# Query tiles of a linear-attention and expert kernel: TensorE's transposes ahead of the projection, ScalarE's exponentials ahead of the projection's copy

## The chip, the cores and the metric

The kernel runs on one core of one Trainium2 chip. The metric is the time of one execution in microseconds. Before the change three runs gave 260.74 us in the median (260.23 to 260.80).

## What is computed

Attention with random features, then a layer of experts. The reference, cut to the part that the change is in:

```python
def phi(x):                                   # x: q or k, scaled; omega is 128 x 64
    proj = np.einsum('bhsd,md->bhsm', x, omega)
    h = proj - np.sum(x * x, axis=-1, keepdims=True) / 2.0
    h = h - np.max(h, axis=-1, keepdims=True)
    return np.exp(h) / np.sqrt(m)
kv  = np.einsum('bhsm,bhsd->bhmd', k_p, v)    # and z, the sum of k_p
num = np.einsum('bhsm,bhmd->bhsd', q_p, kv)
den = np.einsum('bhsm,bhm->bhs', q_p, z)[..., None] + 1e-06
x   = num / den                               # 2304 rows of 8 heads * 64
# then: gate x @ w_gate, one expert of 8 per row, relu(x @ w1[e]) @ w2[e] * gate
```

Sizes: 4 batches, 8 heads, 576 rows each, 128 features; 8 experts, 512 to 1024 to 512.

## The kernel before, in words

One loop (L773) runs 18 key steps (`n < NK`), then 18 query tiles of 128 rows (`t` = 0 to 17), and three more steps in which the last tiles drain. The schedule is manual: on each engine instructions stand in the order in which the Python code issues them, and an engine that waits holds up all that stands behind it. After the loop come the experts: three passes of products each for `relu(x @ w1)` and for `@ w2`, with the operands split into a high and a low part, one expert block after another.

A query tile `t` goes through four steps of the loop:

- Step t. TensorE projects q with omega (`project`, called at L795, matmuls at L177; "P" below): 16 matmuls into two banks of PSUM, heads 4 to 7 in `pj[1]`, heads 0 to 3 in `pj[0]`. VectorE takes maxima of `pj[1]` (L194, called at L863). ScalarE copies `pj[0]` into the SBUF tile `d` (L862), VectorE takes the maxima of that copy (L194, called at L865), GpSimd subtracts them in `d` (L866), and ScalarE writes heads 4 to 7 less their maxima into `d` (L882, four instructions).
- Step t + 2. TensorE transposes `d` (L809, 16 matmuls with the identity; "T" below) into two banks, 3 and 4, under the name `qtr`. ScalarE takes the exponential of each bank (L873, two instructions) into `qpT`.
- Step t + 3. TensorE multiplies `qpT` with the keys' sums `kv_sb` (`numer`, L689, 32 matmuls; "N" below) into `qacc`. This is one pair of banks (tag `a2`, one buffer), so N of the next tile may not begin before VectorE has read this one. `normalise` does that: `den` (L715), a sum of gate products of the tile before (L724), the reciprocal (L718), the product into `xr` (L721). A DMA on SyncE's queue stores `xr` (L727).

So in step t TensorE runs P of tile t, T of tile t - 2, N of tile t - 3, in this order. ScalarE runs copy (t), exponentials (t - 2), L882 (t). VectorE runs maxima of `pj[1]` (t), maxima of `d` (t), `normalise` (t - 3), and in steps 10 to 17 also one transpose of expert rows (`turn_x`, L439). GpSimd subtracts and splits the first expert's weights (L137, L142).

In steps 0 to 5 the last keys' sums are still being finished: `project` first runs a small pair of transposes that waits in the list `beside` (L301, `ktr`), which ScalarE copies out (L305, `kvT`), and after some N a few matmuls give `kv_sb`'s gate columns (L314, copied by VectorE at L322). Such background work hangs on generators that `run(...)` moves on; where a generator yields no name, any `run` call moves it.

The banks that the projection, the transposes and the numerator use (L783, L792, L800, L829):

```python
def pair(name):
    return ps.tile([128, 1024], F32, tag="a2", name=name, bufs=1)
pj = [bank((2 * t + i) % 3, f"pjq{n}{i}") for i in range(2)]
trs = [bank((3 + i, (2, SM)[i])[t > NT], f"qtr{n}{i}") for i in range(2)]
whole = pair(f"qacc{t}")
```

Of the kernel before, what the change touches and what calls it, by code (L numbers as in the profile page):

```python
# [9 lines left out]
F32 = mybir.dt.float32  # L10
# [3 lines left out]
AF = mybir.ActivationFunctionType  # L14
# [5 lines left out]
B, H, S, D, M = 4, 8, 576, 64, 128  # L20
N, DM, E, FF = B * S, H * D, 8, 1024
NP = H // 2
NT = N // 128
# [42 lines left out]
def attention_moe(ctx, tc, kT, qT, va, om, wg, w1, w2, cap, ident, tri, desc, lst, tab0, out):  # L66
    nc = tc.nc
# [12 lines left out]
    def bank(i, name):  # L80
        return ps.tile([128, 512], F32, tag=f"b{i}", name=name, bufs=1)
# [4 lines left out]
    SM = 5  # L86
# [4 lines left out]
    id_sb = const.tile([128, 128], F32, name="id_sb")  # L91
# [61 lines left out]
    def run_one(task):  # L153
        try:
            task[1] = next(task[0])
        except StopIteration:
            tasks.remove(task)

    def run(at=None, times=1, most=99):
        for _ in range(times):  # L160
            for task in list(tasks):
                if task[1] is None or (task[1] == at and most > 0):
                    most -= task[1] is not None
                    run_one(task)
# [9 lines left out]
    def project(parts, banks):  # L174
        def one(k, i):
            rows = slice(64 * i, 64 * i + 64)
            nc.tensor.matmul(banks[i][:, k * M : (k + 1) * M], parts[k][rows, :], om_s[rows, :], start=True, stop=True)  # L177

        a = 0
        if beside:  # L180
            a, small_t = beside.pop(0)
            small_t()
        n = len(parts)
        one(0, 1 - a)
        for k in range(1, n):
            one(k - 1, a)
            one(k, 1 - a)
        one(n - 1, a)
# [16 lines left out]
    qp = qstack.enter_context(tc.tile_pool(name="qpool", bufs=2, side="right"))  # L205
# [564 lines left out]
    ex_l, d_l, qT_l, acc_l = {}, {}, {}, {}  # L770
    step = [0]

    for n in range(NK + NT + 3):  # L773
        t = step[0] = n - NK
        mx = small.tile([128, H], F32, tag="mx", name=f"mx{n}", bufs=4) if n < NK + NT else None

        if n < NK:
            keys = [chunks[b, g][0][:, u * 128 : (u + 1) * 128] for b, g, u in KU[KG * n : KG * n + KG]]
            if n == 0:

                pj = [bank(i, f"pjk{n}{i}") for i in range(4)]
                project(keys[0:2], pj[0:2])
                project(keys[2:4], pj[2:4])  # L783
            else:

                if n == 1:
                    pj = [bank(SM, "pjk10"), pair("pjk11")[:, 0:512]]
                else:
                    pj = [bank(2 * (n % 2) + i, f"pjk{n}{i}") for i in range(2)]
                project(keys, pj)  # L790
        elif t < NT:
            pj = [bank((2 * t + i) % 3, f"pjq{n}{i}") for i in range(2)]  # L792
            c = max(i for i in range(len(QB) - 1) if QB[i] <= t)
            o = (t - QB[c]) * 128
            project([qc[c][:, p, o : o + 128] for p in range(NP)], pj)  # L795
        run("T")

        if 0 <= t - 2 < NT:
            d = d_l.pop(t - 2)
            trs = [bank((3 + i, (2, SM)[i])[t > NT], f"qtr{n}{i}") for i in range(2)]  # L800

            parts = [
                [(trs[i][:, u * 64 : (u + 1) * 64], d[64 * i : 64 * i + 64, u, :], i) for u in range(H)] for i in range(2)
            ]

            for x in chain(*zip_longest(*parts)):
                if x is not None:
                    rows = slice(64 * x[2], 64 * x[2] + 64)
                    nc.tensor.transpose(x[0], x[1], id_sb[rows, rows])  # L809
        if t == NT:  # L810
            h0 = h_tiles()
        run()

        if 0 <= n - 2 < NK:
            ex = ex_l.pop(n - 2)
            for k, (b, g, u) in enumerate(KU[KG * (n - 2) : KG * (n - 1)]):
                if u == 0:
                    if acc_l.get("kp") is None:
                        acc_l["kp"] = pair("kp")
                    acc_l[0] = bank(4, f"kacc{b}{g}") if g == 0 else acc_l["kp"]  # L820
                kv_acc(b, g, u, ex, k, acc_l[0])
                if u == 8:
                    start(kv_gate(b, g, acc_l[0]))
        elif 0 <= t - 3 < NT:
            acc_l["kp"] = whole = None
            if t in (NT, NT + 2):
                acc_l[0] = [bank(3 * (t > NT) + i, f"qacc{t}{i}") for i in range(2)]
            else:
                whole = pair(f"qacc{t}")  # L829
                acc_l[0] = [whole[:, 0:512], whole[:, 512:1024]]  # L830
            numer(t - 3, qT_l.pop(t - 3), acc_l[0])
        run("N")
        if t == NT + 2:
            turn[0] = 2
            take = mm1(*AHEAD[0], *h0, "i0")

        if n < NK:
            ex = kp.tile([128, H, M], F32, tag="ex", name=f"ex{n}", bufs=3)

            for o, q in ((0, pj[0:2]), (2, pj[2:4])) if n == 0 else ((0, pj),):  # L840
                w = KG // (len(pj) // 2)
                maxima_of(mx, o, units(q[0])[:, 0:w, :])
                run()
                feeds(n, 0, mx[:, o : o + 1])
                for k in range(w):
                    nc.scalar.activation(  # L846
                        ex[:, o + k, :], q[0][:, k * M : (k + 1) * M], AF.Exp, bias=mx[:, o + k : o + k + 1], scale=1.0
                    )
                maxima_of(mx, 4 + o, units(q[1])[:, 0:w, :])
                run()  # L850
                feeds(n, 1, mx[:, 4 + o : 5 + o])
                h = slice(4 + o, 4 + o + w)
                nc.vector.tensor_tensor(
                    ex[:, h, :], units(q[1])[:, 0:w, :], mx[:, h].unsqueeze(2).to_broadcast([128, w, M]), op=ALU.add
                )
                nc.scalar.activation(ex[:, h, :], ex[:, h, :], AF.Exp)
            ex_l[n] = ex
            run()
        else:
            if t < NT:  # L860
                d = qp.tile([128, H, M], F32, tag="d", name=f"d{t}", bufs=3)
                nc.scalar.copy(d[:, 0:4, :], units(pj[0]))  # L862
                maxima(mx, 1, units(pj[1]))  # L863
                run()
                maxima(mx, 0, d[:, 0:4, :])  # L865
                nc.gpsimd.tensor_tensor(d[:, 0:4, :], d[:, 0:4, :], spread(mx, 0), op=ALU.add)  # L866
                feeds(n, 0, mx[:, 0:1])
                d_l[t] = d
            run("P", times=2, most=0 if t == 17 else 1 if t in EARLY_SPLIT or t == 16 else 2)
            if 0 <= t - 2 < NT:  # L870
                qpT = qp.tile([128, 2, H * 64], F32, tag="qpT", name=f"qpT{t}", bufs=2)
                for i in range(2):
                    nc.scalar.activation(qpT[:, i, :], trs[i], AF.Exp)  # L873
                qT_l[t - 2] = qpT
                run()
            if t == NT + 2:
                take()
            if t > NT:
                split_x()
            if t < NT:  # L880
                for k in range(4):
                    nc.scalar.activation(  # L882
                        d[:, 4 + k, :], pj[1][:, k * M : (k + 1) * M], AF.Identity, bias=mx[:, 4 + k : 5 + k], scale=1.0
                    )
                run()
            for task in [x for x in tasks if x[1] == "G"]:
                run_one(task)
            if 0 <= t - 3 < NT:
                normalise(t - 3, acc_l[0], whole)
                if t == 3:  # L890
                    start(first_item())
            if t in EARLY_AT:
                b0 = EARLY_AT.index(t)
                turn_x(b0, b0 + 1, b0)
            if t in EARLY_SPLIT:
                split_early(EARLY_SPLIT.index(t))
            if t in (NT, NT + 1):

                b0 = NBA + 5 * (t - NT)
                split_x = turn_x(b0, b0 + 5, b0 - NBA, nc.gpsimd)  # L900
            run(times=3)
        run("E")

        if n == NK + 1:
            kstack.close()
            open_experts()
        if n == 3:
            start(setup())
        if t in (5, 6):
            load_x(slice(0, 32 * NBA), 0, NBA, range(2 * t - 10, 2 * t - 8))  # L910
        if t in FIRST_LOAD:
            i = 2 * FIRST_LOAD.index(t)
            load_x(slice(32 * NBA, SLOTS), NBA, NB, range(i, i + 2))
# [318 lines left out]
```

## Time and profile before

| | before |
|---|---|
| median of 3 runs | 260.74 us (260.23 to 260.80) |
| the profiled execution | 259.68 us, its span 257.9 us |
| TensorE busy | 252.2 us (98%) |
| its weight loads | 231.4 us (90%) |
| VectorE, ScalarE, GpSimd busy | 165.9, 147.7, 49.4 us |
| granted TensorE clock, mean | 0.997 of 2.4 GHz |

The query tiles take the stretch from about 46 to 100 us of the span; the experts follow. An engine's busy time counts an instruction from its start to its last write; the next one on the engine can start before that, so the distance between two starts is what an instruction takes of its engine, and it is often shorter than its duration. In the timeline a row is one instruction or a few alike in a row, with start, duration and, in brackets, how long the engine stood idle before it and what ended that.

### The profile page before, as it was taken

How to read it: one execution, taken by the hardware profiler on the slowest of the kernel's cores; microseconds unless marked ns; L12 is line 12 of the kernel's file. 1: busy time of each engine (PE TensorE's matmuls, PEld its weight loads, DVE VectorE, ACT ScalarE, POOL GpSimd, SP SyncE). 2: the span in 40 equal slices, each digit the busy share in tenths (PEclk: the TensorE clock that was granted, in tenths of full speed). 3: DMA queues.
4: the chain of work that ended last, by engine and by line, in shares of the span. 5: the costliest groups of instructions: out<-in, count | busy, mean ns of one | idle time of the engine just before them, and what ended most of it. 6: DMA issues, size and time to landing. Idle time of an engine off the chain costs nothing. (4 is left out here: it accounts for less than half of the span.)

```text
span 257.9 us, 7657 instructions
## 1 busy us (share of the span) xinstructions
PE 252.2 (98%) x3042; PEld 231.4 (90%) x3042; DVE 165.9 (64%) x355; ACT 147.7 (57%) x370; POOL 49.4 (19%) x95
## 2 busy tenths in 40 slices
PE   7999999999999999999999999999999999999993
PEld 6999999999999999999988889999888999988882
DVE  2999888779899999554853656566750064667500
ACT  3888878899999995327301645552361155524511
POOL 1015111243989986200000000000000000000000
PEclk9999999999999999999999999999999999999998
DMA  7998997544788657790079527992013998850221
GB/s 216 397 325 252 333 341 207 180 123 140 242 247 270 202 202 243 252 346 1 0 150 293 178 84 252 228 274 92 3 42 101 291 215 270 271 159 0 61 85 44
DMA packets 37507, 49.06 MB, mean 190 GB/s; under 512 B 2578, under 2 KB 24722, under 8 KB 37458
## 3 DMA queue, kind: packets, MB, share of 16 engines
q1 hardware_dynamic: 36338, 46.91, 59.8%
q10 hardware_dynamic: 1120, 1.52, 1.8%
q8 instruction: 28, 0.46, 0.7%
q14 instruction: 21, 0.17, 0.2%
HBM read 36.49 MB, written 11.93 MB: 188 GB/s over the span
## 5 line engine op out<-in xcount | busy, mean ns | idle before, releaser
L742 PE MATMUL hi<-xhi,w1hi 128*128 128x256 f32 (+1 forms) x192 | 56.7, 295 | 0.0
L743 PE MATMUL hi<-xhi,w1lo 128*128 128x256 f32 (+1 forms) x192 | 56.4, 294 | 0.0
L744 PE MATMUL hi<-xlo,w1hi 128*128 128x256 f32 (+1 forms) x192 | 56.3, 293 | 0.0
L755 DVE SCALAR_TENSOR_TENSOR hlo<-hi,hhi 128x256 fp32r<-128x256 f32 x48 | 20.2, 420 | 43.1 <-ACT hr L753 21.7
L753 ACT ACTIVATE hhi<-hi 128x256 fp32r<-128x256 f32 x48 | 18.4, 385 | 36.7 <-PE hi L744 36.7
L927 PE MATMUL yi<-w2hi,hhi 128*128 128x512 f32 x96 | 37.4, 390 | 0.0
L928 PE MATMUL yi<-w2hi,hlo 128*128 128x512 f32 x96 | 37.4, 389 | 0.0
L742 PEld LDWEIGHTS hi<-xhi,w1hi 128*128 128x128 f32 x192 | 36.0, 188 | 0.3
L743 PEld LDWEIGHTS hi<-xhi,w1lo 128*128 128x128 f32 x192 | 36.0, 188 | 0.1
L744 PEld LDWEIGHTS hi<-xlo,w1hi 128*128 128x128 f32 x192 | 36.0, 187 | 0.0
L194 DVE TENSOR_REDUCE mx<-pjk 128x4 f32<-128x512 f32 (+1 forms) x38 | 23.4, 656 | 4.2 <-PE pjk L177 4.2
L846 ACT ACTIVATE ex<-pjk,mx 128x128 f32<-128x128 f32 x72 | 20.7, 368 | 5.9 <-DVE mx L194 5.6
L177 PE MATMUL pjk<-om_s,kraw 64*128 64x128 f32 x288 | 23.6, 297 | 0.4 <-DMA kraw<-kT 0.3
L439 DVE STREAM_TRANSPOSE xt<-xg 128x128 f32<-128x128 f32 (+3 forms) x16 | 19.3, 1205 | 7.0 <-DMA xg<-x_d 7.0
L933 PE MATMUL yi<-w2lo,hhi 128*128 128x512 f32 x96 | 23.7, 389 | 0.0
L689 PE MATMUL qacc<-kv_sb,qpT 128*64 128x73 f32 x576 | 22.5, 230 | 0.0
L177 PEld LDWEIGHTS pjk<-om_s,kraw 64*128 64x128 f32 x288 | 20.0, 200 | 1.7 <-DMA kraw<-kT 0.6
L927 PEld LDWEIGHTS yi<-w2hi,hhi 128*128 128x128 f32 x96 | 18.0, 188 | 3.8 <-issue 0.2
L933 PEld LDWEIGHTS yi<-w2lo,hhi 128*128 128x128 f32 x96 | 18.0, 188 | 3.7
L866 POOL TENSOR_TENSOR d<-d,mx 128x512 f32<-128x512 f32 x18 | 18.7, 1041 | 13.4 <-DVE mx L194 9.8
L928 PEld LDWEIGHTS yi<-w2hi,hlo 128*128 128x128 f32 x96 | 18.0, 188 | 3.6
L882 ACT ACTIVATE d<-pjq,mx 128x128 f32<-128x128 f32 x72 | 21.0, 404 | 0.3 <-DVE mx L194 0.3
(154 smaller groups left out, 420.7 us busy)
## 6 DMA issues: line engine op xcount, KB each, us to landing
w1raw<-w SPq DMA_DIRECT2D x16, 512.0 KB, 7.8
w2raw<-w SPq DMA_DIRECT2D x16, 512.0 KB, 4.7
x_d<-xr SPq DMA_DIRECT2D x18, 256.0 KB, 3.2
xg<-x_d SPq DMA_DIRECT2D x12, 288.0 KB, 8.1
v<-va SPq DMA_DIRECT2D x8, 325.0 KB, 4.5
kraw<-kT SPq DMA_DIRECT2D x8, 288.0 KB, 5.5
out<-ysi SPq DMA_DIRECT2D x9, 256.0 KB, 2.1
v<-va SPq DMA_DIRECT2D x3, 650.0 KB, 7.0
```

Source lines behind the costliest of these rows:

```text
L177: nc.tensor.matmul(banks[i][:, k * M : (k + 1) * M], parts[k][rows, :], om_s[rows, :], start=True, stop=True)
L194: nc.vector.tensor_reduce(mx[:, a : a + src.shape[1]], src, op=ALU.max, axis=AX.X, negate=True)
L689: nc.tensor.matmul(acc[i][r : r + 64, p * ROW : (p + 1) * ROW], qpT[:, r // 64, (4 * i + p) * 64 : (4 * i + p) * 64 + 64], kv_sb[(t * 128 ...
L742: nc.tensor.matmul(pt, whi_[:, k, fs], xhi[:, k, sl], start=(k == 0), stop=False)
L743: nc.tensor.matmul(pt, wlo_[:, k, fs], xhi[:, k, sl], start=False, stop=False)
L744: nc.tensor.matmul(pt, whi_[:, k, fs], xlo[:, k, sl], start=False, stop=(k == 3))
L755: nc.vector.scalar_tensor_tensor(lo, src, 0.0, hi.bitcast(F32), op0=ALU.max, op1=ALU.subtract)
L846: nc.scalar.activation(ex[:, o + k, :], q[0][:, k * M : (k + 1) * M], AF.Exp, bias=mx[:, o + k : o + k + 1], scale=1.0)
L882: nc.scalar.activation(d[:, 4 + k, :], pj[1][:, k * M : (k + 1) * M], AF.Identity, bias=mx[:, 4 + k : 5 + k], scale=1.0)
L927: nc.tensor.matmul(pt, hhi[:, f, sl], w2_at(w_hi, f), start=(f == 0), stop=False)
L928: nc.tensor.matmul(pt, hlo[:, f, sl], w2_at(w_hi, f), start=False, stop=False)
L933: nc.tensor.matmul(pt, hhi[:, f, sl], w2_at(w_lo, f), start=False, stop=(f == 7))
```

## The change

In each step of a query tile the 16 transposes are issued ahead of the projection, and the two exponentials ahead of ScalarE's copy of the projection. The call of `run()` behind the exponentials goes.

```diff
         mx = small.tile([128, H], F32, tag="mx", name=f"mx{n}", bufs=4) if n < NK + NT else None
 
+        if 0 <= t - 2 < NT:
+            d = d_l.pop(t - 2)
+            trs = [bank((3 + i, (2, SM)[i])[t > NT], f"qtr{n}{i}") for i in range(2)]
...
+                    nc.tensor.transpose(x[0], x[1], id_sb[rows, rows])
         if n < NK:
...
             project([qc[c][:, p, o : o + 128] for p in range(NP)], pj)
         run("T")
 
-        if 0 <= t - 2 < NT:
-            d = d_l.pop(t - 2)
...
-                    nc.tensor.transpose(x[0], x[1], id_sb[rows, rows])
         if t == NT:
...
         else:
+            if 0 <= t - 2 < NT:
+                qpT = qp.tile([128, 2, H * 64], F32, tag="qpT", name=f"qpT{t}", bufs=2)
+                for i in range(2):
+                    nc.scalar.activation(qpT[:, i, :], trs[i], AF.Exp)
+                qT_l[t - 2] = qpT
             if t < NT:
                 d = qp.tile([128, H, M], F32, tag="d", name=f"d{t}", bufs=3)
                 nc.scalar.copy(d[:, 0:4, :], units(pj[0]))
...
             run("P", times=2, most=0 if t == 17 else 1 if t in EARLY_SPLIT or t == 16 else 2)
-            if 0 <= t - 2 < NT:
-                qpT = qp.tile([128, 2, H * 64], F32, tag="qpT", name=f"qpT{t}", bufs=2)
-                for i in range(2):
-                    nc.scalar.activation(qpT[:, i, :], trs[i], AF.Exp)
-                qT_l[t - 2] = qpT
-                run()
             if t == NT + 2:
```

TensorE at the seam between steps 5 and 6, before: the last transposes of step 5, its numerator, the first matmuls of step 6's projection (`pjq`: projection, `qtr`: transposes, `qacc`: numerator).

```order
L809 MATMUL qtr_1285<-id_sb,d_1159 128x64
L809 MATMUL qtr_1286<-id_sb,d_1159 128x64
L689 MATMUL qacc_1303<-kv_sb_72,qpT_1245 64x73 x16
L177 MATMUL pjq_1344<-om_s,qhlo 128x128
L177 MATMUL pjq_1343<-om_s,qhlo 128x128
```

The same place in the changed kernel:

```order
L177 MATMUL pjq_1289<-om_s,qhhi 128x128
L177 MATMUL pjq_1290<-om_s,qhhi 128x128
L689 MATMUL qacc_1303<-kv_sb_72,qpT_1237 64x73 x16
L788 MATMUL qtr_1343<-id_sb,d_1240 128x64
L788 MATMUL qtr_1344<-id_sb,d_1240 128x64
```

The numerator now stands straight behind the projection, and a step opens with the transposes.

ScalarE in steps 2 and 3, the first two with transposes, before (`d<-pjq ... 128x512`: the copy, `qpT`: the exponentials, `d<-pjq,mx`: L882):

```order
L305 COPY kvT_1030<-ktr_1062 128x2x64
L862 COPY d_1096<-pjq_1060 128x512
L873 ACTIVATE qpT_1101<-qtr_1074 128x512
L873 ACTIVATE qpT_1101<-qtr_1075 128x512
L882 ACTIVATE d_1096<-pjq_1061,mx_1059 128x128 x4
L305 COPY kvT_1030<-ktr_1112 128x2x64
L862 COPY d_1159<-pjq_1110 128x512
L873 ACTIVATE qpT_1164<-qtr_1124 128x512
L873 ACTIVATE qpT_1164<-qtr_1125 128x512
L882 ACTIVATE d_1159<-pjq_1111,mx_1109 128x128 x4
```

The same place in the changed kernel:

```order
L305 COPY kvT_1030<-ktr_1080 128x2x64
L863 ACTIVATE qpT_1096<-qtr_1060 128x512
L863 ACTIVATE qpT_1096<-qtr_1061 128x512
L867 COPY d_1099<-pjq_1078 128x512
L881 ACTIVATE d_1099<-pjq_1079,mx_1059 128x128 x4
L305 COPY kvT_1030<-ktr_1130 128x2x64
L863 ACTIVATE qpT_1159<-qtr_1110 128x512
L863 ACTIVATE qpT_1159<-qtr_1111 128x512
L867 COPY d_1162<-pjq_1128 128x512
L881 ACTIVATE d_1162<-pjq_1129,mx_1109 128x128 x4
```

The copy has moved behind both exponentials; the copies of `kvT` still stand first. The instructions of VectorE, GpSimd and SyncE stand in the same order in both kernels, row for row.

## Rows read from the trace of the kernel before

**Rows 1.** The page's busy times; the list of TensorE's waits (total, times, longest)

```profile
PE 252.2 (98%) x3042; PEld 231.4 (90%) x3042; DVE 165.9 (64%) x355; ACT 147.7 (57%) x370; POOL 49.4 (19%) x95
...
PE pjk L177 <- DMA kraw<-kT: 0.3, 1, 0.3
```

**Rows 2.** Windows: busy us (instructions) by engine, clock, DMA share, GB/s, steps 6 to 10

```profile
61.80:75.85 14.05, 14.05 (x332) 13.32 (x328) 12.33 (x31) 12.90 (x36) 10.77 (x13) 1.00 0.82 248
```

**Rows 3.** Timeline of TensorE, step 9: start, us, engine, line, operation

```profile
70.32 1.16 PE L177 MATMUL pjq<-om_s,qhlo 64*128 64x128 f32 x16
71.32 0.66 PE L809 MATMUL qtr<-id_sb,d 64*128 64x64 f32 x16
71.91 1.25 PE L689 MATMUL qacc<-kv_sb,qpT 128*64 128x73 f32 x32
```

**Rows 4.** Timeline of ScalarE, step 9

```profile
71.64 0.59 ACT L862 COPY d<-pjq 128x512 f32<-128x512 f32 x1 [0.16 <-PE pjq L177]
72.12 1.09 ACT L873 ACTIVATE qpT<-qtr 128x512 f32<-128x512 f32 x2
73.08 1.16 ACT L882 ACTIVATE d<-pjq,mx 128x128 f32<-128x128 f32 x4
```

**Rows 5.** Timeline of VectorE, from step 8's normalise to step 9's

```profile
70.44 0.17 DVE L715 TENSOR_SCALAR den<-qacc 128x8 f32<-128x8 f32 x1 [0.26 <-PE qacc L689]
...
70.88 0.77 DVE L721 TENSOR_TENSOR xr<-qacc,rec 128x584 f32<-128x584 f32 x1
71.59 0.69 DVE L194 TENSOR_REDUCE mx<-pjq 128x4 f32<-128x512 f32 x1
72.25 0.69 DVE L194 TENSOR_REDUCE mx<-d 128x4 f32<-128x512 f32 x1
73.20 0.17 DVE L715 TENSOR_SCALAR den<-qacc 128x8 f32<-128x8 f32 x1 [0.26 <-PE qacc L689]
```

**Rows 6.** Timeline of VectorE and TensorE, step 5: a numerator that follows `xr`

```profile
59.76 0.77 DVE L721 TENSOR_TENSOR xr<-qacc,rec 128x584 f32<-128x584 f32 x1
...
59.94 0.72 PE L809 MATMUL qtr<-id_sb,d 64*128 64x64 f32 x15
60.67 1.25 PE L689 MATMUL qacc<-kv_sb,qpT 128*64 128x73 f32 x32
```

**Rows 7.** Timeline of ScalarE, steps 2 and 3

```profile
52.02 0.29 ACT L305 COPY kvT<-ktr 128x128 f32<-128x128 f32 x1
52.20 0.60 ACT L862 COPY d<-pjq 128x512 f32<-128x512 f32 x1
...
53.66 1.16 ACT L882 ACTIVATE d<-pjq,mx 128x128 f32<-128x128 f32 x4
54.66 0.31 ACT L305 COPY kvT<-ktr 128x128 f32<-128x128 f32 x1
54.81 0.65 ACT L862 COPY d<-pjq 128x512 f32<-128x512 f32 x1
```

**Rows 8.** Timeline of VectorE, step 3, and TensorE's numerator in step 4

```profile
55.49 0.69 DVE L194 TENSOR_REDUCE mx<-d 128x4 f32<-128x512 f32 x1 [0.50 <-ACT d L862]
56.10 0.15 DVE L715 TENSOR_SCALAR den<-qacc 128x8 f32<-128x8 f32 x1
...
56.52 0.77 DVE L721 TENSOR_TENSOR xr<-qacc,rec 128x584 f32<-128x584 f32 x1
...
57.51 1.25 PE L689 MATMUL qacc<-kv_sb,qpT 128*64 128x73 f32 x32
```

**Rows 9.** Timeline, step 12: VectorE's extra transpose; step 9's subtraction on GpSimd

```profile
82.61 0.41 DVE L439 STREAM_TRANSPOSE xt<-xg 128x128 f32<-128x128 f32 x1
...
74.06 1.04 POOL L866 TENSOR_TENSOR d<-d,mx 128x512 f32<-128x512 f32 x1
```

**Rows 10.** Timeline of ScalarE and TensorE, steps 17 and 18

```profile
94.21 1.09 ACT L873 ACTIVATE qpT<-qtr 128x512 f32<-128x512 f32 x2
...
95.18 0.89 PE L809 MATMUL qtr<-id_sb,d 64*128 64x64 f32 x16
```

More of the change, by code (lines that the diff above doesn't have):

```diff
@@ L775, in attention_moe @@
         mx = small.tile([128, H], F32, tag="mx", name=f"mx{n}", bufs=4) if n < NK + NT else None
+        if 0 <= t - 2 < NT:
+            d = d_l.pop(t - 2)
+            trs = [bank((3 + i, (2, SM)[i])[t > NT], f"qtr{n}{i}") for i in range(2)]
+            parts = [
+                [(trs[i][:, u * 64 : (u + 1) * 64], d[64 * i : 64 * i + 64, u, :], i) for u in range(H)] for i in range(2)
+            ]
+            for x in chain(*zip_longest(*parts)):
+                if x is not None:
+                    rows = slice(64 * x[2], 64 * x[2] + 64)
+                    nc.tensor.transpose(x[0], x[1], id_sb[rows, rows])
         if n < NK:
@@ L796, in attention_moe @@
         run("T")
-        if 0 <= t - 2 < NT:
-            d = d_l.pop(t - 2)
[L800 to L808, printed above, removed]
-                    nc.tensor.transpose(x[0], x[1], id_sb[rows, rows])
         if t == NT:
```

## Prediction

> **What bounds the kernel now.** I read the page first, then TensorE's waits, then the timelines of one step. TensorE is busy 252.2 of 257.9 us, and the longest wait its list names after the start is 0.3 us, for a load [rows 1]. So the end moves by what TensorE loses or gains, and I follow the four engines through one query step to see which of the others could hold it up.
>
> Step 9 is typical. TensorE starts the projection P at 70.32, the transposes T at 71.32, the numerator N at 71.91 [rows 3]. P therefore takes 1.00 us of the engine and T 0.59. One step lasts 2.76 us, from one `den` to the next (73.20 - 70.44) [rows 5], which leaves N 1.17. ScalarE's copy comes 1.32 us after P's start, having waited for P [rows 4]; the two exponentials take 0.96 (73.08 - 72.12). VectorE starts the maxima of `pj[1]` at 71.59, 1.27 after P, those of the copy 0.61 after the copy's start, then idles 0.26 until N, which had begun 1.29 before, lets `den` go; `xr` starts 0.44 after `den` (70.88 - 70.44) [rows 4, 5].
>
> The tight place is `qacc`, a single pair of banks: N may not begin before `xr` of the tile before has been read out. Step 5 shows the price of that hand-over: fifteen of the sixteen transposes begin at 59.94 and should let N go near 60.5, but it goes at 60.67, which is 0.91 after `xr`'s start [rows 6]. In step 9 that rule gives 70.88 + 0.91 = 71.79, and N starts at 71.91 [rows 3, 5]: 0.12 us to spare.
>
> **The change, part by part.** Nothing is added or removed on an engine but the place of 16 transposes and two exponentials. VectorE, GpSimd and SyncE keep their order, DMA issues included. The `run()` that goes was one of about eleven calls in a step; the load of the first expert's weights that it moved on is issued a call later, before the same store on SyncE. I cost that at nothing.
>
> *The steady steps.* P now starts 0.59 later in the step, N at the same place. All that VectorE does comes after P, and the early start of the exponentials helps no one: N wants them a whole step later. Count from P's start: copy 1.32, its maxima +0.61, `den` +0.61 (from one such start to `den`'s, 56.10 - 55.49) [rows 8], `xr` +0.44, N of the next step +0.91: 3.89 us. That N is due at 2.76 + 1.00 = 3.76. So N waits 0.13. The wait delays the next step's P but not this one's chain, so the following N finds the 0.13 made good: a wait of 0.13 in every second step, 0.065 a step. VectorE's idle 0.26 is what absorbs the rest of the 0.59. Steps 7 to 17 are 11: **+0.7 us**.
>
> Two covers must hold. VectorE's transposes of expert rows (0.41) [rows 9] follow `xr`: 1.32 + 0.61 + 0.61 + 0.44 + 0.71 + 0.41 = 4.10 after P, and the next maxima are due at 2.76 + 0.065 + 1.27 = 4.10: just covered. On ScalarE, L882 waits for the maxima (1.27 + 0.69), takes 1.00 (54.66 - 53.66) [rows 7], the exponentials 0.96, so the next copy could start 3.92 after P, and is due at 4.08: 0.16 of cover. GpSimd's latest subtraction ends at 75.10 [rows 9], and the transposes of that tile would open step 11 at 70.32 + 2 * 2.76 = 75.84: 0.74 of cover.
>
> *The first steps.* In steps 2 and 3 ScalarE has no slack, as copies of `kvT` stand in its row. Today the copy of step 2 starts at 52.20, straight behind `kvT` [rows 7]. After the change the exponentials stand there: 52.20 to 53.16; then the copy (0.48, 72.12 - 71.64) [rows 4], L882 1.00, `kvT` 0.15 (54.81 - 54.66) [rows 7]: 54.79; the exponentials of step 3: 55.75; its copy starts there in place of 54.81, 0.94 later. Then +0.61 its maxima, +0.61 `den`, +0.42 `xr` (56.52 - 56.10), +0.91: N of step 4 at 58.30 in place of 57.51 [rows 8]. **+0.8 us**, the largest single term. In steps 5 and 6 I expect the small wait of 0.1 before N to go [rows 6] and one of the steady kind (0.13) to come: 0.
>
> *The drain.* T of step 18 takes 0.89 where 0.66 is usual [rows 3, 10]: its banks are still read by exponentials that start at 94.21 and last 1.09. These now run before the copy, about 1 us earlier. **-0.2 us**.
>
> Sum: 0.8 + 0.7 - 0.2 = +1.3 us. TensorE shows no wait afterwards, so I let the delay run through to the end. The profiled execution took 259.68, which becomes 261.0. It lies 1.06 under the median of the runs, so on that basis 260.74 + 1.3 = **262.0 us**.
>
> Bounds. Each hand-over between engines was read once or twice, and a chain of five may be 0.12 shorter (then the steady steps cost nothing) or 0.15 longer (0.28 in every second step: 1.5). The first steps: 0.4 if `kvT`'s copies come through earlier, 1.0 if the small transposes, now behind T, hold them back. The drain 0 to -0.3. Ends: +0.1 and +2.5. I take 1.3, as the value straight from the rows.
>
> A page speaks to whether TensorE, busy all the time, could yet get shorter. In steps 6 to 10 its weight loads cover 13.32 of 14.05 us, 0.73 short of all, at full granted clock [rows 2]. The Trainium skill (Perfetto Trace Analysis, section Identifying the Most-Contended Engine) holds that busy time of matmuls is a poor measure of how near TensorE is to its limit, and that of weight loads a good one. By that rule some 0.15 us a step is still to be had by another order. The rows show no seam that a swap would close: P, T and N each keep one pitch, and the same instructions stand in each step.
>
> **Rivals.**
> - *No measurable difference* (within 0.2%, 0.5 us, about what a measurement can tell). `qacc` is read out in time: the chain after P is under 3.76 rather than 3.89, and ScalarE catches up in steps 2 and 3. For it: only 0.13 decides the steady part. Against: the first steps' delay is a plain sum of ScalarE's own durations, with no hand-over that I could have misread by 0.3. Time: 260.9.
> - *ScalarE's ring closes.* Maxima, L882, exponentials, next copy: a cover of 0.16 a step. Records of the copy reach 0.65 in step 3 against 0.59 [rows 4, 7]; if the ring is 0.1 over, all 11 steps lose that: 1.1 more, 263.1.
> - *Faster.* TensorE packs T, P, N closer than P, T, N, and the uncovered 0.73 us of five steps [rows 2] shrinks. It decides if the seam in front of T costs less than that behind P today. All of it in 16 steps with transposes is 2.3 us: 258.4; a quarter is 260.2. For it: only that share. Against: the pitch above; nothing else on TensorE's path gets shorter but the drain's 0.2.
> - That the change does not do what it says is excluded by the order of both engines.
>
> **How the numbers follow.** Forecast 0.58, ScalarE's ring 0.14, no difference 0.21, faster 0.07. Slower by over 0.2% is the sum of the first two, 0.72. The forecast's own bounds reach from 260.8 to 263.2; the range takes in most of the no-difference case: 260.5 to 263.2.
>
> **What would show it.** Right: TensorE's wait list names `qacc` for `xr` (L721); N of step 4 starts 0.8 us late; steps alternate between about 2.76 and 2.9 us; VectorE's 0.26 before `den` is gone in the steps without a transpose of expert rows; T of step 18 takes 0.66. Wrong: steps of 2.76 throughout, and experts that begin no later than before. If the steps are longer than 2.9, look at whether the copy waits for the exponentials rather than for P: that is the ring.

## The result, and the profile after

| | before | after |
|---|---|---|
| median of 22 runs each | 260.43 us (259.00 to 263.04) | 262.03 us (259.94 to 264.00) |
| ratio | | 1.0053 [1.0031, 1.0075] |
| profiled execution, its span | 259.68, 257.9 us | 261.79, 260.0 us |
| query stretch in it | 49.41 us | 50.36 us |

The changed kernel is slower by half a per cent: the ratio on 260.43 is +1.4 us, from +0.8 to +2.0. Forecast were +1.3 us and 262.0. The ratios here and below leave out runs that are over 1.5% above the fastest of their kernel, while the medians and ranges have all runs.

"Query stretch" means here and below: from TensorE's first instruction of step 2, the first step with transposes, to the experts' first product (L742, at 100.29 us before and 102.45 after). The rest of the span behind it is 157.6 us in both (257.9 - 100.29; 260.0 - 102.45). In front of it the profiled execution of after lost 1.2 us (step 2 opens at 52.09, before at 50.88). That is not the change's, since steps 0 and 1 hold no transposes. Over the profiles of all kernels below step 2 opens anywhere from 50.2 to 52.1 us, in either order, and the list of TensorE's waits puts 0.9 us of this one down to the keys' loads (the first row, 1.2; in [rows 1] 0.3):

```profile
PE pjk L177 <- DMA kraw<-kT: 1.2, 2, 0.8
...
PE qacc L689 <- DVE xr L721: 0.4, 1, 0.4
```

The last row is new: once, for 0.4 us, a numerator waits for `xr`. The page's busy times are nearly those of [rows 1], and the instructions are as many:

```profile
PE 252.4 (97%) x3042; PEld 230.3 (89%) x3042; DVE 166.6 (64%) x355; ACT 148.7 (57%) x370; POOL 49.2 (19%) x95
```

So I look for the 0.95 us of the query stretch by the starts of the numerators, counted from the start of step 2 (us; N of the first tile is in step 3):

| N in step | 3 | 4 | 5 | 6 | 7 | 10 | 11 | 17 | 18 | L742 |
|---|---|---|---|---|---|---|---|---|---|---|
| before | 3.75 | 6.63 | 9.79 | 12.55 | 15.50 | 23.80 | 26.56 | 43.12 | 45.12 | 49.41 |
| after | 4.17 | 7.51 | 10.74 | 13.51 | 16.47 | 24.78 | 27.64 | 44.25 | 46.07 | 50.36 |
| later by | 0.42 | 0.88 | 0.95 | 0.96 | 0.97 | 0.98 | 1.08 | 1.13 | 0.95 | 0.95 |

**0.96 us is lost by step 6**, 0.88 of it by step 4. From step 6 to step 17 only 0.17 more goes, of which 0.10 in one step; the drain gives 0.18 back.

*Steps 2 to 4.* The timeline of after, ScalarE, VectorE and TensorE (start, duration, engine, line, operation; in brackets the idle time before it and what ended that):

```profile
53.22 0.29 ACT L305 COPY kvT<-ktr 128x128 f32<-128x128 f32 x1
53.37 1.12 ACT L863 ACTIVATE qpT<-qtr 128x512 f32<-128x512 f32 x2
54.34 0.63 ACT L867 COPY d<-pjq 128x512 f32<-128x512 f32 x1
54.80 1.21 ACT L881 ACTIVATE d<-pjq,mx 128x128 f32<-128x128 f32 x4
55.81 0.35 ACT L305 COPY kvT<-ktr 128x128 f32<-128x128 f32 x1
55.96 1.20 ACT L863 ACTIVATE qpT<-qtr 128x512 f32<-128x512 f32 x2
56.92 0.70 ACT L867 COPY d<-pjq 128x512 f32<-128x512 f32 x1
...
57.66 0.69 DVE L194 TENSOR_REDUCE mx<-d 128x4 f32<-128x512 f32 x1 [0.55 <-ACT d L867]
58.26 0.16 DVE L715 TENSOR_SCALAR den<-qacc 128x8 f32<-128x8 f32 x1
...
58.69 0.77 DVE L721 TENSOR_TENSOR xr<-qacc,rec 128x584 f32<-128x584 f32 x1
...
54.14 1.12 PE L788 MATMUL qtr<-id_sb,d 64*128 64x64 f32 x16
...
59.60 1.25 PE L689 MATMUL qacc<-kv_sb,qpT 128*64 128x73 f32 x32 [0.38 <-DVE xr L721]
```

ScalarE has no idle time from 53.22 to the end of step 3's copy; the row is the one that the prediction wrote down (53.22 + 0.15 + 0.97 + 0.46 + 1.01 + 0.15 + 0.96 = 56.92). That copy starts 4.83 us after step 2 (56.92 - 52.09), before 3.93 ([rows 7], 54.81 - 50.88): 0.90 later. Its maxima follow after 0.74 (VectorE stood idle for it), `den` after 0.60, `xr` after 0.43, N after 0.91. Step 3's transposes at 54.14 take 0.90 us of TensorE instead of the 0.55 they take later (the projection's next row starts at 55.04): they write the banks that the exponentials from 53.37 to 54.49 still read. That wait is 0.35 of the 0.42 of step 3; it comes out of the same ScalarE row and is not added to the 0.88, since N of step 4 would otherwise only have waited longer for `xr`.

*A steady step*, the timeline of the same three engines, from one `xr` to the next numerator but one:

```profile
73.19 0.77 DVE L721 TENSOR_TENSOR xr<-qacc,rec 128x584 f32<-128x584 f32 x1
74.28 0.69 DVE L194 TENSOR_REDUCE mx<-pjq 128x4 f32<-128x512 f32 x1 [0.32 <-PE pjq L177]
74.92 0.69 DVE L194 TENSOR_REDUCE mx<-d 128x4 f32<-128x512 f32 x1
75.53 0.16 DVE L715 TENSOR_SCALAR den<-qacc 128x8 f32<-128x8 f32 x1
...
75.96 0.77 DVE L721 TENSOR_TENSOR xr<-qacc,rec 128x584 f32<-128x584 f32 x1
...
72.23 1.14 ACT L881 ACTIVATE d<-pjq,mx 128x128 f32<-128x128 f32 x4
73.32 1.08 ACT L863 ACTIVATE qpT<-qtr 128x512 f32<-128x512 f32 x2
74.31 0.58 ACT L867 COPY d<-pjq 128x512 f32<-128x512 f32 x1
...
72.51 0.71 PE L788 MATMUL qtr<-id_sb,d 64*128 64x64 f32 x16
73.06 1.11 PE L177 MATMUL pjq<-om_s,qhlo 64*128 64x128 f32 x16
74.10 1.25 PE L689 MATMUL qacc<-kv_sb,qpT 128*64 128x73 f32 x32
75.28 0.71 PE L788 MATMUL qtr<-id_sb,d 64*128 64x64 f32 x16
75.83 1.11 PE L177 MATMUL pjq<-om_s,qhlo 64*128 64x128 f32 x16
76.87 1.25 PE L689 MATMUL qacc<-kv_sb,qpT 128*64 128x73 f32 x32
```

T takes 0.55, P 1.04, N 1.18: 2.77 us, before 2.76. Both numerators start exactly 0.91 us after an `xr` (73.19 to 74.10, 75.96 to 76.87), the distance of [rows 6]. No wait is listed, since none is left over: `xr` comes just in time. VectorE's 0.26 us before `den` [rows 5] is gone; its idle time now lies before the maxima of `pj[1]`, 0.32.

*Step 10*, 0.10 us longer than the rest (timeline of GpSimd and TensorE):

```profile
76.04 1.04 POOL L137 TENSOR_SCALAR w1hi<-w1raw 128x1024 fp32r<-128x1024 f32 x1 [1.40 <-DMA w1raw<-w]
77.05 1.04 POOL L871 TENSOR_TENSOR d<-d,mx 128x512 f32<-128x512 f32 x1
...
78.14 0.71 PE L788 MATMUL qtr<-id_sb,d 64*128 64x64 f32 x16
```

GpSimd waited 1.40 us for a load of the expert's weights, with step 9's subtraction queued behind; its end (78.09) and the transposes that read it (78.14) stand 0.05 apart. The pitch of 2.77 would have put them at 78.05. Before, GpSimd waited for the same load too, and TensorE lost nothing by it:

```profile
73.06 1.05 POOL L137 TENSOR_SCALAR w1hi<-w1raw 128x1024 fp32r<-128x1024 f32 x1 [1.07 <-DMA w1raw<-w]
```

The call of `run()` that went has not delayed the load: SyncE issues it 0.71 us behind N of step 7 (69.27 - 68.56), before 0.85 (67.23 - 66.38). It landed later: GpSimd could start 6.77 us after the issue (76.04 - 69.27), before 5.83.

*The drain.* T of step 18 lasts 0.71 in place of 0.89 [rows 10]:

```profile
97.52 0.71 PE L788 MATMUL qtr<-id_sb,d 64*128 64x64 f32 x16
98.16 1.25 PE L689 MATMUL qacc<-kv_sb,qpT 128*64 128x73 f32 x32
```

### The profile page after: what moved, and what is told of

Its sections match the earlier page's. It is cut to its first block, busy times and chain, and to the rows that moved or that the text cites. A ratio compares the mean times of both kernels' runs of the same rounds, so it can differ in the third digit from the quotient of the medians.

```text
span 260.0 us, 7659 instructions
## 1 busy us (share of the span) xinstructions
PE 252.4 (97%) x3042; PEld 230.3 (89%) x3042; DVE 166.6 (64%) x355; ACT 148.7 (57%) x370; POOL 49.2 (19%) x95
## 5 line engine op out<-in xcount | busy, mean ns | idle before, releaser
L742 PE MATMUL hi<-xhi,w1hi 128*128 128x256 f32 (+1 forms) x192 | 56.7, 296 | 0.0
L755 DVE SCALAR_TENSOR_TENSOR hlo<-hi,hhi 128x256 fp32r<-128x256 f32 x48 | 20.2, 420 | 43.2 <-ACT hr L753 21.9
L742 PEld LDWEIGHTS hi<-xhi,w1hi 128*128 128x128 f32 x192 | 36.0, 188 | 0.3
L689 PEld LDWEIGHTS qacc<-kv_sb,qpT 128*64 128x64 f32 x576 | 19.9, 136 | 2.6 <-PE pjq L177 0.8
L881 ACT ACTIVATE d<-pjq,mx 128x128 f32<-128x128 f32 x72 | 20.7, 381 | 1.9 <-DVE mx L194 0.6
```

Source lines behind the costliest of these rows:

```text
L689: nc.tensor.matmul(acc[i][r : r + 64, p * ROW : (p + 1) * ROW], qpT[:, r // 64, (4 * i + p) * 64 : (4 * i + p) * 64 + 64], kv_sb[(t * 128 ...
L742: nc.tensor.matmul(pt, whi_[:, k, fs], xhi[:, k, sl], start=(k == 0), stop=False)
L755: nc.vector.scalar_tensor_tensor(lo, src, 0.0, hi.bitcast(F32), op0=ALU.max, op1=ALU.subtract)
L881: nc.scalar.activation(d[:, 4 + k, :], pj[1][:, k * M : (k + 1) * M], AF.Identity, bias=mx[:, 4 + k : 5 + k], scale=1.0)
```

## Experiments

My theory: the loss is made in steps 2 to 5, by ScalarE's row (the exponentials ahead of the copy, with the copies of `kvT`) through `xr` and `qacc`; later steps stand at the edge and cost next to nothing; the drain gives 0.2 back. The rivals: the steady steps pay (0.065 each, the prediction's own term), or GpSimd's late subtractions do.

### Where the loss is: the new order in some steps only

The code of both orders stands in the kernel, and a table of steps chooses (`E_FIRST` guards the exponentials likewise). Beside them the change was run once more.

```diff
+T_FIRST = range(0, 6)        # first_only; range(6, 30) in from_6
+E_FIRST = range(0, 6)
...
+        if 0 <= t - 2 < NT and t in T_FIRST:
+            d = d_l.pop(t - 2)
...
-        if 0 <= t - 2 < NT:
+        if 0 <= t - 2 < NT and t not in T_FIRST:
```

> The changed kernel once more, as the measure for the other three. Query stretch = from TensorE's first instruction of step 2 to the experts' first product: 49.4 us before, 50.4 in the first profile of the changed kernel. Theory A (the loss is ScalarE's row in steps 2 to 4: +0.9, the later steps sit just at the edge of the qacc hand-over and lose under 0.1 in all, the drain gives back 0.2) expects 50.2 to 50.5 again, with N of step 4 late and steps of 2.77 from 7 on. Theory B (the later steps lose 0.065 each, as predicted, and the first profile only hid it) expects 50.7 to 51.1. Time against before: +1.3 us (+0.5%).

> The new order in steps 2 to 5 alone, the old one from step 6 on. Theory A: all the loss is here and the drain's gain is not, stretch 50.2 to 50.5, time +1.0 us (+0.4%). Theory B: stretch 50.2 too, so this run alone does not tell them apart, only together with the one that has the new order from step 6 on.

> The new order from step 6 on, the old one in steps 2 to 5. Theory A: the first steps' loss is gone and the drain's gain stays, stretch 49.2 to 49.5, time within 0.2% of before. Theory B: the later steps still lose, stretch 49.8 to 50.0, time +0.5 us (+0.2%).

> The new order from step 6 on once more: its first profile had a gap of 0.8 us inside the transposes of step 9 for which the profile shows no wait, and two later steps that waited for GpSimd, while its timed runs were 0.3% under before. If the gap belonged to that one execution, the stretch is now 49.2 to 50.0 and the time 0 to 0.4% under before. If it belongs to the order, the stretch is 51 again and the time no lower than before.

Measured (12 runs each, beside 35 of before; the second set on another occasion, with 35 runs of before of its own):

| kernel | median, us | ratio to before | query stretch |
|---|---|---|---|
| the change again | 262.51 | 1.0077 [1.0040, 1.0115] | 50.62 |
| new order in steps 2 to 5 | 262.04 | 1.0046 [1.0013, 1.0078] | 50.37 |
| new order from step 6 | 260.45 | 0.9967 [0.9937, 0.9998] | 51.37 |
| the same, second set | 260.04 | 0.9991 [0.9959, 1.0023] | 49.47 |

The first four steps alone bring the loss of the profiles (50.37 against 50.36 in after), and the other fourteen bring none. The timed runs agree with that, though their intervals are too wide to tell 1.0046 from 1.0077. In the kernel with the new order in steps 2 to 5, N of step 4 stands at 7.51 after step 2's start, as in after; its line numbers are shifted by two:

```profile
59.46 1.25 PE L691 MATMUL qacc<-kv_sb,qpT 128*64 128x73 f32 x32 [0.38 <-DVE xr L723]
```

From step 6 on its pitch is 2.76, as before. The kernel from step 6 keeps N of step 4 at 6.62, pays 0.19 in step 6, where the orders change over (3.14 between numerators, before 2.95), then runs at 2.77, and gets 0.18 back in the drain (N of step 17 to N of step 18 takes 1.82, before 2.00). Its first profile had 51.37 because of three long steps: TensorE once stood still for 0.82 us with no wait that the trace names (3.86 from N of step 9 to the next), and lost more behind N of steps 11 and 13 (3.05, 3.28). The second profile had none of these (last section). Its timed runs were 0.3% under before in the first set, where I had expected 0.2% at most.

The profile of the change repeated has N of step 4 at 7.52 and step 10 longer by 0.15, with GpSimd again waiting for the load (1.45), and one more step by 0.15 (2.92 from N of step 13 to the next; last section).

### What the first steps pay for: `kvT`'s copies off ScalarE

```diff
-            nc.scalar.copy(
+            (nc.scalar.copy if step[0] < 2 else nc.vector.tensor_copy)(
```

> The changed kernel with the kvT copies of steps 2 to 5 on VectorE instead of ScalarE. Theory A: ScalarE's row gets shorter by 0.15 us each in steps 2 and 3, so N of step 4 is 0.3 earlier, stretch 49.9 to 50.1. Rival: the delay in steps 3 and 4 comes from the transposes that wait for the exponentials of the step before to leave their banks, whatever stands before them, and VectorE's copies only move the wait: stretch 50.3 or more.

Measured: 262.44 us, ratio 1.0056 [1.0022, 1.0090], stretch 50.87. Where it acts, the edit did what the theory says: step 3's copy starts 4.53 us after step 2 (4.83 in after), N of step 4 at 7.18 (7.51), with a wait of 0.21 in place of 0.38. In the whole it missed: by step 8 the gain was gone. ScalarE's exponentials of step 7 began late (the first row; 1.09 after their transposes, 0.81 elsewhere), with them the copy, and N of step 8 waited again. Two later steps were long as well: N of step 12 stands 0.91 behind a late `xr` (2.97 from the N before it), and the transposes of step 14 started late (3.18).

```profile
67.27 1.08 ACT L863 ACTIVATE qpT<-qtr 128x512 f32<-128x512 f32 x2 [0.41 <-PE qtr L788]
70.81 1.25 PE L689 MATMUL qacc<-kv_sb,qpT 128*64 128x73 f32 x32 [0.20 <-DVE xr L721]
81.17 0.77 DVE L721 TENSOR_TENSOR xr<-qacc,rec 128x584 f32<-128x584 f32 x1 [0.24 <-DVE rec L718]
82.08 1.25 PE L689 MATMUL qacc<-kv_sb,qpT 128*64 128x73 f32 x32
83.89 1.04 POOL L871 TENSOR_TENSOR d<-d,mx 128x512 f32<-128x512 f32 x1
86.44 0.71 PE L788 MATMUL qtr<-id_sb,d 64*128 64x64 f32 x16 [0.35 <-POOL w1lo L142]
```

The last row names GpSimd, but the subtraction that these transposes need (the row above) had ended 1.51 us before them, and in after the same transposes start (86.45) while that `w1lo` still runs (85.99 to 87.41). So this is not a wait for GpSimd (last section).

So `kvT` is over a third of the loss at N of step 4 (0.33 of 0.88). The rest I put down to the order itself; no run takes it apart. The tile that was early here did not stay so.

### Each half alone

> Only TensorE's half of the change: transposes first, ScalarE's copy still ahead of the exponentials. Theory: the exponentials now start 1.25 + 0.48 after P and end 1.1 later, and the next step's transposes, which open it, wait for them to leave their two banks: about 2.9 after P, where they are due at 2.2, so every step loses about 0.6 and the stretch grows by some 9 us to 58. Rival (the hand-over of qacc is the only tight place, and it is no tighter here): stretch 50 to 51.

> Only ScalarE's half: exponentials ahead of the copy, TensorE's transposes still behind the projection. Theory: the copy now waits for transposes and exponentials, 2.77 after P instead of 1.32, and with it the maxima, normalise and the release of qacc: N of the next step 5.3 after P where it is due at 4.35; two steps take 5.3 + 1.2 = 6.5, so 3.25 a step, and the stretch grows by 6 to 8 us. Rival (the order on ScalarE matters in the first steps alone): stretch 50 to 51.

`T_FIRST = range(0, 30)` with `E_FIRST = ()`, and the reverse. One run each, beside before at 260.47: 270.38 us (stretch 59.8) and 270.52 us (stretch 58.9). Both are slower by 9.9 and 10.1 us, more than I expected of either. Transposes first, with the copy still ahead of the exponentials (TensorE and ScalarE):

```profile
74.58 0.71 PE L790 MATMUL qtr<-id_sb,d 64*128 64x64 f32 x15 [0.20 <-ACT qpT L892]
76.39 0.58 ACT L881 COPY d<-pjq 128x512 f32<-128x512 f32 x1 [0.84 <-PE pjq L179]
```

The copy waits for P, the exponentials stand behind it, and the next step's transposes wait until these have left their banks: 3.44 us a step (74.58 to 78.02). Exponentials first, with the transposes still behind P:

```profile
74.24 1.25 PE L691 MATMUL qacc<-kv_sb,qpT 128*64 128x73 f32 x32 [0.27 <-DVE xr L723]
75.69 1.16 PE L179 MATMUL pjq<-om_s,qhlo 64*128 64x128 f32 x16 [0.20 <-ACT d L881]
74.07 1.09 ACT L877 ACTIVATE qpT<-qtr 128x512 f32<-128x512 f32 x2 [0.77 <-PE qtr L823]
```

Here ScalarE waits for T with the copy queued behind, so `xr` is late for N, and P is late too, since the copy still reads its bank; this second wait is what I had not counted. 3.37 us a step (74.24 to 77.61). Each half alone costs some 10 us, where both together cost 1.4.

### Is there slack left in the hand-over?

> The changed kernel with one more reciprocal of 128x8 (about 0.2 us of VectorE, its result unused) just before den in steps 6 to 9. Theory A: these steps sit at the edge of the hand-over, N starts 0.91 after xr in each, so the probe shows at once: steps 7 to 10 lose about 0.1 each, 0.4 in all. Rival: VectorE's idle 0.33 before the maxima takes it in, and the steps stay at 2.77.

> The same probe in the kernel before. Theory A: there VectorE idles 0.26 until N lets den go, the probe falls into that, and steps 6 to 9 stay at 2.76, the stretch at 49.4. Rival: steps lengthen as in the changed kernel.

In both kernels one small operation that nothing reads stands ahead of `den` in four steps:

```diff
+        if 3 <= t <= 6:
+            nc.vector.reciprocal(probe, probe)
```

One run each: 260.15 us after, 259.63 us before (the unprobed before: 260.47). The numerators of after behind the probes are 3.00, 2.80, 2.80, 2.80 us apart, against 2.96, 2.77, 2.77, 2.77: 0.13 us in all. Before keeps 2.76 in the last three of these steps, and its stretch (49.43). In the first, where VectorE also copies gate columns (L322), it loses 0.06 too (3.01 against 2.95): there N stands 0.92 behind `xr` (64.85 to 65.77). So in the steady steps before has slack and after has none; but the size was wrong, 0.4 expected. The rows of after show why: `den` starts 0.72 after the maxima began (67.68 to 68.40) in place of 0.61, but `xr` follows it after 0.38 in place of 0.43, so the chain from P to N is 0.06 longer, 3.87. And a wait w of N counts twice on the way to the next N, in the step and in the projection's place: 2.77 + w + 1.04 + w = 3.87, so w = 0.03, as measured, in every step and not in every second one.

```profile
67.68 0.69 DVE L194 TENSOR_REDUCE mx<-d 128x4 f32<-128x512 f32 x1
68.29 0.19 DVE L717 RECIPROCAL probe<-probe 128x8 f32<-128x8 f32 x1
68.40 0.12 DVE L719 TENSOR_SCALAR den<-qacc 128x8 f32<-128x8 f32 x1
...
68.78 0.77 DVE L725 TENSOR_TENSOR xr<-qacc,rec 128x584 f32<-128x584 f32 x1
```

### The drain

Before, with the transposes of step 18 in banks that no exponential reads at that time:

```diff
-            trs = [bank((3 + i, (2, SM)[i])[t > NT], f"qtr{n}{i}") for i in range(2)]
+            trs = [bank(((SM, 3)[i] if t == NT else 3 + i, (2, SM)[i])[t > NT], f"qtr{n}{i}") for i in range(2)]
```

> The kernel before, with the transposes of step 18 alone in other banks (5 and 3 in place of 3 and 4), which the exponentials of step 17 leave earlier. Theory: the drain's 0.2 us was that bank wait, so the transposes of step 18 take 0.66 in place of 0.89 and the stretch is 49.2. Rival: the exponentials' order itself gave it, stretch 49.4. Time within 0.2% either way.

Measured: 261.16 us, ratio 1.0004 [0.9967, 1.0041]. The transposes last 0.71, and N of step 17 to N of step 18 takes 1.83, as in after:

```profile
96.54 0.71 PE L809 MATMUL qtr<-id_sb,d 64*128 64x64 f32 x16
97.19 1.25 PE L689 MATMUL qacc<-kv_sb,qpT 128*64 128x73 f32 x32
```

The bank is the cause in that place. The whole run shows nothing of it: 0.17 us is under what the timing resolves, and this profile's stretch is 51.21, with a stop of 1.04 us elsewhere (last section).

### The expert's loads a step earlier

> The same with the first expert's three later weight loads issued one step earlier (steps 5, 7, 9 in place of 6, 8, 10). Theory: the transposes, which now open a step, are due 1 us earlier than before, and GpSimd, held up before its subtraction by a weight split that waits for its load (1.4 us in the changed kernel's profile), is at times late for them; with earlier loads that wait goes, no step after the sixth is over 2.8, and the stretch is 49.2 to 49.4, time 0.3% under before. Rival: the waits for GpSimd come from its own backlog (its busy share is near 1 in steps 9 to 16), so late steps stay, 49.5 to 50.5.

> The kernel before with the same earlier loads, as a control. Theory: there the transposes come 1 us later in the step and the load's wait is covered, so stretch 49.4 and time within 0.2% of before. Rival: earlier loads help by themselves, time 0.2% or more under before.

```diff
-W1_LOADS = (0, 6, 8, 10)
+W1_LOADS = (0, 5, 7, 9)
```

With the new order from step 6: 260.51 us, ratio 1.0004 [0.9974, 1.0034], stretch 49.48, no wait of GpSimd for the weights. With the order before: 260.13 us, 0.9996 [0.9972, 1.0021], stretch 49.40. Neither gains. The wait in step 10 goes, but in a kernel whose second profile (49.47) did not pay for it either. GpSimd's late subtraction is thus a matter of when a load lands, not of the order alone. No version here is shown to be faster than before: of the two sets of the order from step 6, one's interval ends just under 1 and the other's holds 1.

## Why the prediction was right, and where not

- **The sign and the size**: right. 262.0 was forecast, 262.03 measured. That they agree to 0.03 is luck: before has a median of 260.43 and not 260.74, the largest error of a term was 0.6, and some 0.4 us of the timed difference were found in no step. Of the terms, two came within 0.2, one was much too large, and a cover that I had costed at nothing gave way.
- **The first steps, +0.8**: 0.88 at N of step 4, and 0.96 by step 6. The mechanism held instruction by instruction: the copy 0.90 late (0.94 forecast), N waiting for `xr`. Not foreseen: that T of step 3 waits for the exponentials' banks, which costs nothing beside the rest. "In steps 5 and 6: 0" was 0.08. The runs with the new order in some steps only show that the loss is made here.
- **The steady steps, +0.7**: mis-sized; over steps 7 to 17 the pitch went from 2.76 to 2.77, some 0.07 us in all. The chain from P was read as 3.89 against 3.76 due. It is 1.25 (copy) + 0.61 + 0.61 + 0.43 + 0.91 = 3.81, against 2.77 + 1.04 = 3.81. The copy was read 0.07 too late (1.32, [rows 3, 4]); now it starts with the end of the exponentials, 0.99 behind their start, and these 0.81 behind T. Most of the 0.07 goes with P itself: its 16 matmuls last 1.11 us in after and 1.16 before, and VectorE's maxima of `pj[1]`, which wait for P, stand 1.22 behind its start in after, but 1.27 in the kernel with TensorE's half alone, where they wait too and P lasts 1.17. And P takes 0.04 more of TensorE in its new place, and T 0.04 less. The forecast of alternating steps of 2.76 and 2.9 was wrong with it; that the slack is used up was right, as the probes show. More than half of the forecast sum of 1.3 was this term.
- **The drain, -0.2**: -0.18, by the bank, which the old order with other banks shows as well.
- **The covers**: VectorE's held. ScalarE's, put at 0.16, is 0.08 (L881 from 72.23 takes 1.01, the exponentials start at 73.32), and it held, so the ring of the second rival did not close. GpSimd's 0.74 came from a single subtraction [rows 9]. It did not hold where a load of weights landed late: 0.10 in this profile, 0.15 in the repeat.
- **TensorE packing closer** (rival, 0.07): in five steps of after weight loads cover 13.08 of 14.04 us (window from N of step 5 to N of step 10, columns as in [rows 2]), before 13.32 of 14.01 in the matching window (60.67 to 74.68). What they leave uncovered grew from 0.69 to 0.96, and N of step 5 to N of step 10 takes 14.04 in place of 14.01 (table above). By the prediction's estimate the rule of the Trainium skill (Perfetto Trace Analysis, Identifying the Most-Contended Engine) left 0.15 us a step to be had; this order did not get it.

```profile
62.83:76.87 14.04, 14.04 (x329) 13.08 (x329) 12.26 (x31) 13.36 (x36) 8.79 (x10) 1.00 0.75 222
```

- The profiled terms sum to 0.95, and the timed runs give 1.4, with 0.8 as lower end. The repeat gave +2.0 (1.0 to 3.0). All that I could place in steps lies between 0.95 and 1.2; whether the rest is scatter or something that these profiles did not catch stays open. One candidate is the stops of the last section, but twelve profiles don't tell whether they come more often in the new order.

## What to carry to other kernels

Moving work ahead in one engine's row helps only if what then stands behind it has slack, and that must be counted in the steps where the row is fullest: the loss here was made in four steps with extra copies in ScalarE's row, not in the eleven alike that a page's average shows. A hand-over, read as the distance of two starts, can change by some hundredths with the order that it is to forecast (the copy behind P: 1.32 before, 1.25 after); chains of several of them, compared with a due time 0.1 us away, don't give a sign. And two rows that feed each other, as transposes and exponentials here, must be swapped together or not at all.

## What the runs showed of the hardware

**TensorE stops for 0.8 to 1.0 us with no wait named**, in two of the twelve profiles of this study that are not of the half changes, one of either order in those steps: the drain kernel in the middle of a projection, and the first run of the kernel from step 6 in the middle of its transposes. Each stands after the fifth instruction of its group:

```profile
74.10 0.82 PE L177 MATMUL pjq<-om_s,qhlo 64*128 64x128 f32 x10 [1.04 <-issue]
```

```profile
75.30 0.59 PE L790 MATMUL qtr<-id_sb,d 64*128 64x64 f32 x11 [0.82 <-issue]
```

The granted clock was 1.00 there. The trace has a candidate, the DMA queue that carries instructions, here in a window of 0.1 us of the drain kernel from 71.4 (packets, MB, share of 16 engines):

```profile
q8 instruction: 1, 0.02, 84.6%
```

That share of 0.1 us of 16 engines is 1.35 us of packet time; the packet lands by about 72.8, and TensorE goes on 1.3 us later. In the other kernel the packet starts just before 73.0, takes 1.07 us, and TensorE goes on 1.3 us after its end, too. In both the packet begins 21.2 to 21.3 us after step 2's start, and in the ten other profiles 18.6 to 20.2 us after it, with no stop.

Two packets later the queue shows the same. In four profiles it begins 32.1 to 33.0 us after step 2's start, and in each of them TensorE loses time 1.3 to 1.5 us behind its end: 0.15 us in the repeat of the change, within the numerator of step 13 (the row below; 1.25 elsewhere), 0.41 in the `kvT` kernel and 0.51 in the first run from step 6, both at the transposes of step 14, and 0.20 in the drain kernel. In the eight others it begins 29.6 to 31.4 us after step 2's start, and none of them loses anything there. GpSimd, which the profile names at the two starts of transposes, had done what these need 1.5 to 1.7 us before. The packet between the two begins at 25.7 and 25.9 us in the two kernels that stopped, with 0.28 and 0.37 us lost 1.3 to 1.5 us behind its end, and by 24.6 us in the ten others, with no loss.

```profile
84.24 1.40 PE L689 MATMUL qacc<-kv_sb,qpT 128*64 128x73 f32 x32
```

So TensorE seems to have run out of instructions where a packet came late. No run tested that by an edit, and why these packets start later in some executions stays open.
